# Fused attention and two MoE blocks: the x-combinations of the second block made one per product, a chunk ahead

## The chip, the cores and the metric

The kernel runs on one core of one Trainium2 chip. The metric is the device time of one execution in microseconds (us); the kernel before takes 1987.3 us, the median of three runs (1986.35 to 1988.73).

## The reference

```python
x = attention(q, k, v, p)              # 2304 tokens x 512, packed through 32 proxies
h = x @ w_in;  x = (h * cos(h)) @ w_out            # block 1, d_ff = 2048
P = sinkhorn(exp(x @ w_gate))                      # 2304 x 8, eight rounds
out = sum over e of P[:, e] * (relu(x @ w1[e]) @ w2[e])   # block 2: 8 experts, 1024 wide
```

All in float32. Each matrix is held as a rounded high part (`xh`, type fp32r) and a low part (`xl`, the difference), and every product is three matrix products (high*high, high*low, low*high).

## The kernel before, in words

Everything is transposed: features on the 128 partitions, tokens along the free dimension. After attention, block 1 runs as 64 steps `s` (four units of 16), written out in a fixed order: `in_front` and `in_back` issue for each step 12 matmuls of the first product (`in_g1`), the cosine on ScalarE (ACT) and VectorE (DVE) (`in_turns`, `in_rest`, `in_sin`, `in_square`, `in_g`), the split of h into high (`in_hi`, ACT) and low (`in_lo`, GpSimd, called POOL), the 24 matmuls of the second product for the step three before (`in_g2`), and its addition into the SBUF accumulator (`in_acc`, DVE, line 573). There are four pairs of PSUM banks, two for each product, so `in_g2(j)` waits for `in_acc(j-2)`.

Block 2 runs as 16 units (expert and half); u = 4 (`U1`) is the first. Tokens are cut into four chunks j of 512 columns (plus a rest, j = 4). In a chunk the first product uses a Strassen-Winograd scheme with seven products m in the order (0, 5, 1, 6, 4, 3, 2), each of 12 matmuls (`g1_mult`, line 723). They need seven combinations of blocks of x per chunk: m = 0, 1, 2 are plain blocks, m = 4, 5, 6, 3 are differences. `x_make(j, qs)` makes them: a subtraction on DVE (line 624), the high part on ACT (line 615), the low part on DVE or POOL (line 616), in staging slots (`slot_of`, 256-column pieces of `xh` and `xl` that block 1 no longer reads), and stores both parts to a DRAM tensor `xd` by two DMAs of the SP queue (line 618). `x_load` (line 656) loads the parts of a product from `xd` into a ring of four slots (0 to 3); it is called behind each product for the one four later, first four times ahead of the chunk loop. All 16 units read `xd`. The four blocks of w1 of a unit are combined and split in the same manner by `w1_make` on ACT and POOL (lines 678, 679, 682).

The generators are stepped by hand. In the kernel before, `x_make(0)` and `x_make(1)` are both stepped within steps 56 to 63 of block 1 and emptied behind them; `x_make(2)` and `x_make(3)` within chunk 0 and early chunk 1 of the first unit. Between the products of a chunk stand the second products: in chunk 0 of u = 4 the last three `in_g2` of block 1 (steps 61 to 63), then four `out_g2` per chunk (12 matmuls each, lines 827 to 829) of the chunk before. "Side" work, stepped by `step_side`, is the gate: `logits(c)` (matmuls line 863, copies 867 and 868, transposes 871, reduction 855, all in PSUM bank 7), and then `sinkhorn`. An engine's instructions run in the order in which they are written here.

Of the kernel before, what the change touches and what calls it, by code (L numbers as in the profile page):

```python
# [8 lines left out]
F32 = mybir.dt.float32  # L9
# [5 lines left out]
ALU = mybir.AluOpType  # L15
# [16 lines left out]
NJ = 4  # L32
# [71 lines left out]
def tile_kernel(ctx: ExitStack, tc: tile.TileContext, qT, kT, v, pT, w_in, w_out, w_gate, w1, w2, out):  # L104
# [496 lines left out]

    def x_make(j, qs):

        b11, b12 = x_block(0, 2 * j), x_block(0, 2 * j + 1)
        b21, b22 = x_block(1, 2 * j), x_block(1, 2 * j + 1)
        n = 0

        def tmp():
            return temp("tx").rearrange("p (a n) -> p a n", a=2)

        def put(m, src, eng):
            nonlocal n
            hi, lo = slot_of(qs[n % len(qs)])
            n += 1
            nc.scalar.copy(hi, src)  # L615
            eng.tensor_tensor(out=lo, in0=src, in1=hi.bitcast(F32), op=ALU.subtract)  # L616
            for i, part in enumerate((hi, lo)):
                nc.sync.dma_start(
                    out=xd[7 * j + m, :, i, :].rearrange("p (a n) -> p a n", a=2),
                    in_=part.bitcast(F32),  # L620
                )

        def sub(out, a, b):
            nc.vector.tensor_tensor(out=out, in0=a, in1=b, op=ALU.subtract)  # L624

        t1 = tmp()
        sub(t1, b12, b11)
        put(0, b11, nc.gpsimd)
        yield
        t2 = tmp()  # L630
        sub(t2, b22, t1)
        put(5, t2, nc.vector)
        yield
        put(1, b21, nc.gpsimd)
        put(4, t1, nc.vector)
        yield
        t3 = tmp()
        sub(t3, b22, b12)
        put(6, t3, nc.vector)
        yield  # L640
        t4 = tmp()
        sub(t4, b21, t2)
        put(3, t4, nc.vector)
        yield
        put(2, b22, nc.gpsimd)

    x_seq = [7 * j + m for j in range(NJ) for m in MULTS]
    counts = {"load": 0, "use": 0, "bank": 0, "slot": 0}

# [15 lines left out]
    def w1_make(u, early, late):  # L665
        def tile_():
            return wp.tile([P, 512], F32, tag="w1h", name="wraw")

        a11, a12, a21, a22 = (tile_() for _ in range(4))
        for i, t in enumerate((a11, a12, a21, a22)):  # L670
# [14 lines left out]
        put(0, a11, early[0])  # L685
        s1, s2 = tile_(), tile_()
        comb(s1, a21, a22, ALU.add)
# [242 lines left out]
    with tc.manual_schedule():  # L930
# [137 lines left out]

        def step_tail(n=1):
            for _ in range(n):  # L1070
                while tail:
                    try:
                        next(tail[0])
                        break
                    except StopIteration:
                        tail.pop(0)

        spare, late = [4, 5, 6, 7], [8, 9, 10, 11]
        preps = {U1: w1_make(U1, spare, late)}
        n0 = n1 - 16  # L1080
        for s in range(NPLAN, n1):
            in_front(s)
            in_back(s)
            if s == n0 + 4:
                w2_load(U1)
            if s == n0 + 7:
                next(preps[U1])
                w2_split(U1, 0)
            if s == n0 + 8:
                w2_split(U1, 1)  # L1090
                tail.append(x_make(0, range(4)))
            if s == n0 + 12:
                tail.append(x_make(1, range(4)))
            if n0 + 8 <= s < n0 + 15:
                step_tail(2)
            if n0 + 8 <= s < n0 + 13:
                next(preps[U1])
            if n0 + 13 <= s:
                next(preps[U1], None)
        step_tail(20)  # L1100
        next(preps[U1], None)
        for _ in range(4):
            x_load()
        tail.append(x_make(2, range(12, 16)))
        in_hi(n1 - 1)
# [9 lines left out]

        spare, late = [12, 13, 14, 15], [5, 7, 8, 10]
        prev = None
        for u in range(U1, NU):
            for j in range(NJ + 1):
                if prev is None:  # L1120
                    def last(i):
                        in_g2(i)
                        in_acc(i)
                        if i == n1 - 1:
                            tail.append(x_make(3, range(12, 16)))
                            side.extend(logits(c) for c in range(8))
                            side.extend([logits_rest(), sinkhorn()])
# [4 lines left out]
                steps = g1_steps(u, j) if j < NJ else g1_rest(u)  # L1132
                places = (1, 2, 3) if prev is None else (1, 3, 4, 5) if j < NJ else (0, 0, 1, 1)
                i = 0
                for n in range(7 if j < NJ else 2):
                    next(steps, None)
                    while i < len(g2) and places[i] == n:
                        g2[i]()
                        i += 1
                    step_tail(2 if prev is None and n < 4 else 1)  # L1140
                    if u > U1 or (j == 0 and n > 3) or (j > 0 and n in (1, 3, 4, 5)):
                        step_side()

                    if j == 0 and n in (3, 5):
                        w2_split(u, 2 + n // 5)
                    if u + 1 < NU:
                        if j == 1 and n == 0:
                            preps[u + 1] = w1_make(u + 1, spare, late)
                            next(preps[u + 1])
                        if j == 2 and n < 5:  # L1150
                            next(preps[u + 1])
# [56 lines left out]
```

## Time and profile before

| what | value |
|---|---|
| median of three runs | 1987.3 us |
| profiled execution | 1988.1 us, its span 1986.3 us |
| TensorE (PE) busy | 1936.6 us (97%), mean granted clock 0.991 |
| DVE, ACT, POOL busy | 961.3, 622.1, 530.1 us |
| DMA | 321.18 MB, mean 162 GB/s, 50.0% of 16 engines |

The span is the time from the first to the last instruction of the core; the execution's own time lies 1.8 us above it. PE busy 97% says that the matrix engine sets the end nearly everywhere, so time can only be won where it waits or where its clock is granted at half. The rows further below are from the 100 us in which block 1 ends and block 2 begins.

### The profile page before, as it was taken

The numbers are of one execution on the slowest core, as the hardware profiler recorded it, in microseconds if no ns is written. First come the engines' busy times: TensorE is split into PE (matmuls) and PEld (weight loads), VectorE is DVE, ScalarE is ACT, GpSimd is POOL, SyncE is SP. The second block draws the span as 40 slices with busy tenths as digits, with TensorE's granted clock in tenths as the row PEclk, the third lists the DMA queues.
The fourth block names the chain that finished last, engine by engine and source line by source line (L and its number), as shares of the span: only waits on it lengthen the run. The fifth ranks groups of instructions, "written<-read, shape, count | busy, mean of one in ns | idle before, by whom it ended". The sixth has DMA issues, their size and how long they took to land.

```text
span 1986.3 us, 32260 instructions
## 1 busy us (share of the span) xinstructions
PE 1936.6 (97%) x13241; PEld 1745.7 (88%) x13241; DVE 961.3 (48%) x1427; ACT 622.1 (31%) x1062; POOL 530.1 (27%) x426
## 2 busy tenths in 40 slices
PE   7999999869999999999999999999999999999998
PEld 4799999857889989998998989989989898989897
DVE  6867776653363554343444343434344444434343
ACT  5877776532321212121222121212111211212110
POOL 3445554642121212121212121213131222212100
PEclk9999999979999999999999999999999999999999
DMA  8411111385363737474646455555546463737373
GB/s 294 149 53 45 54 54 33 127 276 191 118 220 119 227 123 231 129 229 135 221 139 211 158 192 163 187 177 163 191 149 210 130 222 118 233 114 236 117 228 101
DMA packets 290067, 321.18 MB, mean 162 GB/s; under 512 B 18560, under 2 KB 267264, under 8 KB 289920
## 3 DMA queue, kind: packets, MB, share of 16 engines
q1 hardware_dynamic: 289920, 319.12, 50.0%
q8 instruction: 104, 1.70, 0.4%
q14 instruction: 43, 0.35, 0.1%
HBM read 299.65 MB, written 19.40 MB: 161 GB/s over the span
## 4 chain that ended last, share of the span: by engine, by line
PE 77%; DVE 1%; ACT 0%; issue 0%; DMA 0%; POOL 0%; SPq 0%; ACTq 0%
PE bank L723 32%; PE bank L827 13%; PE bank L828 13%; PE bank L829 13%; PE bank L792 5%; PE bank L863 0%; DMA xl<-xd 0%; DVE xl L616 0%; ACT xh L615 0%; DVE tx L624 0%; DVE c L747 0%; ACT hreg L731 0%; DVE lg L855 0%; POOL wlo L221 0%; DVE hreg L732 0%
## 5 line engine op out<-in xcount | busy, mean ns | idle before, releaser
L723 PE MATMUL bank<-xh 128*128 128x256 f32 x1792 | 509.5, 284 | 7.1 <-DMA xh<-xd 7.1
L723 PE MATMUL bank<-xl,xh 128*128 128x256 f32 x1792 | 507.6, 283 | 0.4 <-DMA xl<-xd 0.3
L723 PE MATMUL bank<-xh,xl 128*128 128x256 f32 x1792 | 507.6, 283 | 0.0
L839 DVE SCALAR_TENSOR_TENSOR acc<-bank,prob,acc 128x512 f32<-128x512 f32 (+1 forms) x253 | 189.5, 749 | 364.4 <-PE bank L829 364.1
L723 PEld LDWEIGHTS bank<-xh 128*128 128x128 f32 x1792 | 341.8, 191 | 22.0 <-issue 10.7
L723 PEld LDWEIGHTS bank<-xl,xh 128*128 128x128 f32 x1792 | 341.8, 191 | 10.3 <-DMA xl<-xd 0.9
L679 POOL TENSOR_TENSOR xl<-wraw,xh 128x512 fp32r<-128x512 f32 x128 | 165.1, 1305 | 684.6 <-ACT xh L678 471.4
L723 PEld LDWEIGHTS bank<-xh,xl 128*128 128x128 f32 x1792 | 342.3, 191 | 0.0
L827 PE MATMUL bank<-whi,hreg 128*128 128x512 f32 (+1 forms) x822 | 323.8, 394 | 0.0
L828 PE MATMUL bank<-wlo,hreg 128*128 128x512 f32 (+1 forms) x822 | 323.4, 393 | 0.0
L829 PE MATMUL bank<-whi,hreg 128*128 128x512 f32 (+1 forms) x822 | 322.8, 393 | 0.0
L731 ACT ACTIVATE hreg<-c 128x512 fp32r<-128x512 f32 x137 | 86.6, 632 | 459.7 <-DVE c L747 459.7
L221 POOL TENSOR_TENSOR wlo<-raw,whi 128x512 fp32r<-128x512 f32 x64 | 83.0, 1297 | 464.8 <-ACT whi L220 464.7
L562 PE MATMUL bank<-hreg,whi 128*128 128x288 f32 x1024 | 189.8, 297 | 7.5 <-DVE acc L573 7.0
L829 PEld LDWEIGHTS bank<-whi,hreg 128*128 128x128 f32 x822 | 154.6, 188 | 35.5
L827 PEld LDWEIGHTS bank<-whi,hreg 128*128 128x128 f32 x822 | 154.9, 188 | 28.0
L828 PEld LDWEIGHTS bank<-wlo,hreg 128*128 128x128 f32 x822 | 154.8, 188 | 27.2
L562 PEld LDWEIGHTS bank<-hreg,whi 128*128 128x128 f32 x1024 | 155.2, 191 | 10.2 <-ACT rbuf L524 4.2
L732 DVE SCALAR_TENSOR_TENSOR hreg<-c,hreg 128x512 fp32r<-128x512 f32 x137 | 97.6, 712 | 99.6 <-ACT hreg L731 99.6
L828 PE MATMUL bank<-wlo,slot 128*128 128x512 f32 (+1 forms) x334 | 131.0, 392 | 0.0
L827 PE MATMUL bank<-whi,slot 128*128 128x512 f32 (+1 forms) x334 | 131.0, 392 | 0.0
L829 PE MATMUL bank<-whi,slot 128*128 128x512 f32 (+1 forms) x334 | 130.4, 391 | 0.0
(152 smaller groups left out, 2828.1 us busy)
## 6 DMA issues: line engine op xcount, KB each, us to landing
xh<-xd SPq DMA_DIRECT2D x448, 256.0 KB, 3.4
xl<-xd SPq DMA_DIRECT2D x448, 256.0 KB, 3.8
raw<-w SPq DMA_DIRECT2D x32, 512.0 KB, 6.1
wraw<-w SPq DMA_DIRECT2D x64, 256.0 KB, 5.4
raw<-w_in SPq DMA_DIRECT2D x16, 512.0 KB, 3.8
raw<-w_out SPq DMA_DIRECT2D x16, 512.0 KB, 3.6
xd<-xh SPq DMA_DIRECT2D x28, 256.0 KB, 2.6
xd<-xl SPq DMA_DIRECT2D x28, 256.0 KB, 2.7
```

Source lines behind the costliest of these rows:

```text
L221: nc.gpsimd.tensor_tensor(out=lo, in0=raw, in1=hi.bitcast(F32), op=ALU.subtract)
L562: nc.tensor.matmul(ps[:, di, 0:HC], lhsT=lhsT, rhs=rhs, start=(n in (0, 6)), stop=(n in (17, 23)),)
L679: nc.gpsimd.tensor_tensor(out=lo, in0=src, in1=hi.bitcast(F32), op=ALU.subtract)
L723: nc.tensor.matmul(dst, lhsT=w, rhs=t[:, k, :], start=start and p + k == 0 and w is a and t is th, stop=p + k == 2 and w is bq, skip_group ...
L731: nc.scalar.activation(hi, src, AF.Relu)
L732: nc.vector.scalar_tensor_tensor(out=lo, in0=src, scalar=0.0, in1=hi.bitcast(F32), op0=ALU.max, op1=ALU.subtract)
L792: nc.tensor.matmul(dst, lhsT=w, rhs=t, start=q + k == 0 and w is a and t is th, stop=q == 1 and k == KD - 1 and w is bq, skip_group_check= ...
L827: nc.tensor.matmul(ps, lhsT=a, rhs=wh, start=(f == 0), stop=False)
L828: nc.tensor.matmul(ps, lhsT=a, rhs=wl, start=False, stop=False)
L829: nc.tensor.matmul(ps, lhsT=bq, rhs=wh, start=False, stop=(f == 3))
L839: nc.vector.scalar_tensor_tensor(out=dst, in0=ps, scalar=prob[:, t, e:e + 1], in1=dst, op0=ALU.mult, op1=ALU.add)
```

## The change

`x_make` keeps the same seven combinations, but each of its eight pieces finishes the low part of the product before and issues the next subtraction and high part; all low parts are now on DVE, none on POOL. `x_make(0)` is stepped once per step in steps 56 to 63, with its first four products written straight into ring slots 0 to 3 (they are still stored to `xd`), so that the load counter starts at 4 and the four loads ahead of the chunk loop are gone. `x_make(1)`, `(2)` and `(3)` are stepped one piece per product of chunks 0, 1 and 2 of the first unit, through slots 8 to 11, with their differences in buffers of the pool `wp`. The last four splits of the first `w1_make` move from the end of block 1 to products 0 to 3 of chunk 0, the next unit's `w1_make` from chunks 1 and 2 to chunks 2 and 3. The last three `in_g2` move from products 1, 2, 3 to 1, 3, 5, and in the first unit the side work is stepped at the last product of chunk 0 and then behind every product.

```diff
-    def x_make(j, qs):
+    def x_make(j, qs, tmp):
...
-        def put(m, src, eng):
-            nonlocal n
-            hi, lo = slot_of(qs[n % len(qs)])
-            n += 1
-            nc.scalar.copy(hi, src)
-            eng.tensor_tensor(out=lo, in0=src, in1=hi.bitcast(F32), op=ALU.subtract)
+        src = {0: b11, 1: b21, 2: b22}
+
+        def sub(m, a, b):
+            src[m] = tmp().rearrange("p (a n) -> p a n", a=2)
+            nc.vector.tensor_tensor(out=src[m], in0=a, in1=b, op=ALU.subtract)
+
+        def high(m):
+            nc.scalar.copy(slot_of(qs[m])[0], src[m])
+
+        def low(m):
+            hi, lo = slot_of(qs[m])
+            nc.vector.tensor_tensor(out=lo, in0=src[m], in1=hi.bitcast(F32), op=ALU.subtract)
             for i, part in enumerate((hi, lo)):
                 nc.sync.dma_start(
...
-        t1 = tmp()
-        sub(t1, b12, b11)
-        put(0, b11, nc.gpsimd)
-        yield
-        t2 = tmp()
-        sub(t2, b22, t1)
-        put(5, t2, nc.vector)
-        yield
-        put(1, b21, nc.gpsimd)
-        put(4, t1, nc.vector)
-        yield
...
+        sub(4, b12, b11)
+        high(0)
+        yield
+        low(0)
+        sub(5, b22, src[4])
+        high(4)
+        yield
+        low(4)
+        high(5)
+        yield
+        low(5)
+        sub(6, b22, b12)
+        high(1)
+        yield
+        low(1)
+        sub(3, b21, src[5])
+        high(6)
+        yield
+        low(6)
+        high(3)
+        yield
+        low(3)
+        high(2)
+        yield
+        low(2)
...
-    counts = {"load": 0, "use": 0, "bank": 0, "slot": 0}
+    counts = {"load": 4, "use": 0, "bank": 0, "slot": 0}
...
-        spare, late = [4, 5, 6, 7], [8, 9, 10, 11]
+        direct = {m: (0, 1, 2, 3, 8, 10, 9)[i] for i, m in enumerate(MULTS)}
+        through = {m: 8 + i % 4 for i, m in enumerate((0, 4, 5, 1, 6, 3, 2))}
+
+        def x_temp():
+            return wp.tile([P, 512], F32, tag="w1h", name="tx")
+
+        spare, late = [4, 5, 6, 7], [12, 13, 14, 15]
...
-                tail.append(x_make(0, range(4)))
-            if s == n0 + 12:
-                tail.append(x_make(1, range(4)))
-            if n0 + 8 <= s < n0 + 15:
-                step_tail(2)
+                tail.append(x_make(0, direct, lambda: temp("tx")))
+            if n0 + 8 <= s:
+                step_tail()
             if n0 + 8 <= s < n0 + 13:
                 next(preps[U1])
-            if n0 + 13 <= s:
-                next(preps[U1], None)
-        step_tail(20)
-        next(preps[U1], None)
-        for _ in range(4):
-            x_load()
-        tail.append(x_make(2, range(12, 16)))
...
+                first_unit = u == U1
+                if first_unit and 0 < j + 1 < NJ:
+                    tail.append(x_make(j + 1, through, x_temp))
...
-                            tail.append(x_make(3, range(12, 16)))
...
-                places = (1, 2, 3) if prev is None else (1, 3, 4, 5) if j < NJ else (0, 0, 1, 1)
+                places = (1, 3, 5) if prev is None else (1, 3, 4, 5) if j < NJ else (0, 0, 1, 1)
...
-                    step_tail(2 if prev is None and n < 4 else 1)
-                    if u > U1 or (j == 0 and n > 3) or (j > 0 and n in (1, 3, 4, 5)):
+                    if not first_unit or n == 6 or (j > 0 and n < 6):
                         step_side()
+                    if first_unit:
+                        if j == 0 and n < 4:
+                            next(preps[U1], None)
+                        step_tail()
...
-                        if j == 1 and n == 0:
+                        if (j, n) == ((2, 6) if first_unit else (1, 0)):
                             preps[u + 1] = w1_make(u + 1, spare, late)
                             next(preps[u + 1])
-                        if j == 2 and n < 5:
+                        if j == (3 if first_unit else 2) and first_unit <= n < 5 + first_unit:
                             next(preps[u + 1])
```

In `step_tail` every generator in the list now advances by one piece per call; before, only the first one did. In `w1_make` the six buffers are taken at once, in another order.

## Rows read from the trace of the kernel before

**Rows 1.** Waits, 350 to 450 us: who waited for whom, total us, times, longest.

```profile
PE bank L863 <- DVE lg L855: 7.4, 2, 3.9
PE bank L723 <- DMA xh<-xd: 7.1, 1, 7.1
PE bank L562 <- DVE acc L573: 7.0, 3, 3.2
PE bank L871 <- DVE l_rest L868: 4.6, 1, 4.6
```

**Rows 2.** Windows: length, busy per engine (x count), PEclk, DMA share, GB/s.

```profile
380.00:400.00 20.00, 12.93 (x81) 12.22 (x80) 14.06 (x17) 11.79 (x23) 11.11 (x12) 0.91 0.45 153
400.00:410.00 10.00, 5.57 (x24) 5.30 (x25) 5.15 (x6) 4.83 (x10) 8.70 (x8) 0.53 0.94 303
430.00:440.00 10.00, 5.13 (x24) 3.42 (x24) 4.96 (x11) 1.76 (x3) 1.53 (x2) 0.57 0.98 314
440.00:450.00 10.00, 6.18 (x35) 5.17 (x36) 3.14 (x8) 2.35 (x4) 0.85 (x1) 0.58 0.41 129
```

**Rows 3.** Timeline of PE: start us, us, line; first matmuls of steps 56 and 57.

```profile
347.64 0.29 PE L503 MATMUL bank<-xh 128*128 128x288 f32 x1
352.39 0.29 PE L503 MATMUL bank<-xh 128*128 128x288 f32 x1
```

**Rows 4.** Timeline of PE: chunk 0, its first two products, its third one.

```profile
404.34 0.55 PE L723 MATMUL bank<-xh 128*128 128x256 f32 x1 [7.13 <-DMA xh<-xd]
...
410.06 0.68 PE L562 MATMUL bank<-hreg,whi 128*128 128x288 f32 x2
...
413.61 0.28 PE L723 MATMUL bank<-xh 128*128 128x256 f32 x1
...
415.05 0.43 PE L562 MATMUL bank<-hreg,whi 128*128 128x288 f32 x2
```

**Rows 5.** Timeline of ACT: the copy behind the first product of chunks 1, 2, 3.

```profile
447.97 0.58 ACT L752 COPY ta<-bank 128x512 f32<-128x512 f32 x1 [5.06 <-PE bank L723]
...
475.07 0.59 ACT L752 COPY ta<-bank 128x512 f32<-128x512 f32 x1
...
498.52 0.59 ACT L752 COPY ta<-bank 128x512 f32<-128x512 f32 x1
```

**Rows 6.** Timeline of PE: an output, transposes, logits, next product.

```profile
456.50 0.40 PE L827 MATMUL bank<-whi,slot 128*128 128x512 f32 x1
...
459.27 0.38 PE L871 MATMUL bank<-ident,l_sb 128*128 128x128 f32 x2
459.96 0.69 PE L863 MATMUL bank<-acc,wgs 128*32 128x288 f32 x8 [0.32 <-DVE lg L855]
460.59 0.39 PE L723 MATMUL bank<-xh 128*128 128x256 f32 x1
```

**Rows 7.** Timeline of DVE: a logits copy, a low part behind ACT.

```profile
460.72 0.42 DVE L867 COPY l_sb<-bank 128x256 f32<-128x256 f32 x1 [0.81 <-PE bank L863]
...
463.70 0.69 DVE L732 SCALAR_TENSOR_TENSOR hreg<-c,hreg 128x512 fp32r<-128x512 f32 x1 [0.70 <-ACT hreg L731]
```

**Rows 8.** Lines 616 and 624: duration ns min/median/max, starts, forms.

```profile
L616 DVE TENSOR_TENSOR xl<-tx,xh x16: 691/693/1360, 357.2 to 442.9; 128x512 fp32r<-128x512 f32 x16
L616 POOL TENSOR_TENSOR xl<-acc,xh x12: 1262/1290/1747, 354.2 to 449.1; 128x512 fp32r<-128x512 f32 x12
...
L624 DVE TENSOR_TENSOR tx<-acc x8: 679/1029/1772, 353.1 to 433.1; 128x512 f32<-128x512 f32 x8
```

**Rows 9.** Three-microsecond window with a short wait, columns as in rows 2.

```profile
551.00:554.00 3.00, 1.54 (x13) 1.34 (x12) 2.57 (x8) 0.11 (x1) 0.00 (x0) 1.00 0.88 260
```

**Rows 10.** DMA issues, 410 to 440 us: count, KB each, median us to landing.

```profile
xd<-xl SPq DMA_DIRECT2D x12, 256.0 KB, 3.4
...
xl<-xd SPq DMA_DIRECT2D x6, 256.0 KB, 4.6
```

**Rows 11.** Tile xd, 395 to 470 us: issue to landing.

```profile
DMA to landing us min/median/max: 2.2/4.0/5.7
```

More of the change, by code (lines that the diff above doesn't have):

```diff
@@ L600, in x_block @@
         return cols.rearrange("p (a n) -> p a n", a=2)[:, :, 0:HT]
-    def x_make(j, qs):
+    def x_make(j, qs, tmp):
         b11, b12 = x_block(0, 2 * j), x_block(0, 2 * j + 1)
         b21, b22 = x_block(1, 2 * j), x_block(1, 2 * j + 1)
-        n = 0
-        def tmp():
-            return temp("tx").rearrange("p (a n) -> p a n", a=2)
-        def put(m, src, eng):
-            nonlocal n
-            hi, lo = slot_of(qs[n % len(qs)])
-            n += 1
-            nc.scalar.copy(hi, src)
-            eng.tensor_tensor(out=lo, in0=src, in1=hi.bitcast(F32), op=ALU.subtract)
+        src = {0: b11, 1: b21, 2: b22}
[7 more added lines that the diff above has]
+            nc.vector.tensor_tensor(out=lo, in0=src[m], in1=hi.bitcast(F32), op=ALU.subtract)
             for i, part in enumerate((hi, lo)):
@@ L621, in put @@
                 )
-        def sub(out, a, b):
-            nc.vector.tensor_tensor(out=out, in0=a, in1=b, op=ALU.subtract)
-        t1 = tmp()
-        sub(t1, b12, b11)
-        put(0, b11, nc.gpsimd)
+        sub(4, b12, b11)
+        high(0)
         yield
-        t2 = tmp()
-        sub(t2, b22, t1)
-        put(5, t2, nc.vector)
+        low(0)
+        sub(5, b22, src[4])
+        high(4)
         yield
-        put(1, b21, nc.gpsimd)
-        put(4, t1, nc.vector)
+        low(4)
+        high(5)
         yield
-        t3 = tmp()
-        sub(t3, b22, b12)
-        put(6, t3, nc.vector)
+        low(5)
+        sub(6, b22, b12)
+        high(1)
         yield
-        t4 = tmp()
-        sub(t4, b21, t2)
-        put(3, t4, nc.vector)
+        low(1)
+        sub(3, b21, src[5])
+        high(6)
         yield
-        put(2, b22, nc.gpsimd)
+        low(6)
[5 more added lines that the diff above has]
+        low(2)
     x_seq = [7 * j + m for j in range(NJ) for m in MULTS]
-    counts = {"load": 0, "use": 0, "bank": 0, "slot": 0}
+    counts = {"load": 4, "use": 0, "bank": 0, "slot": 0}
     def x_load():
@@ L667, in tile_ @@
             return wp.tile([P, 512], F32, tag="w1h", name="wraw")
-        a11, a12, a21, a22 = (tile_() for _ in range(4))
+        a11, s2, s1, a22, a12, a21 = (tile_() for _ in range(6))
         for i, t in enumerate((a11, a12, a21, a22)):
@@ L685, in w1_make @@
         put(0, a11, early[0])
-        s1, s2 = tile_(), tile_()
         comb(s1, a21, a22, ALU.add)
@@ L1067, in tile_kernel, with step_tail @@
         tail = []
[L1069 to L1076, printed above, removed]
-        spare, late = [4, 5, 6, 7], [8, 9, 10, 11]
+        def step_tail():
+            for make in list(tail):
+                if next(make, "end") == "end":
+                    tail.remove(make)
+        direct = {m: (0, 1, 2, 3, 8, 10, 9)[i] for i, m in enumerate(MULTS)}
[3 more added lines that the diff above has]
+        spare, late = [4, 5, 6, 7], [12, 13, 14, 15]
         preps = {U1: w1_make(U1, spare, late)}
@@ L1113, in tile_kernel @@
         l_rest = op.tile([P, 2 * P], F32, name="l_rest")
-        spare, late = [12, 13, 14, 15], [5, 7, 8, 10]
+        spare, late = [8, 9, 10, 11], [5, 7, 12, 14]
         prev = None
```

## The prediction

> **What bounds the kernel now.** I read the page first: PE is busy 97% of the span, and the row of granted clock over 40 slices is short of full only at the start and in slices 7 and 8, 347 to 447 us, where block 1 turns into block 2. So I asked only there, in this order: the waits of PE, the windows with the clock, then the timelines of PE, DVE and ACT side by side.
>
> The waits [rows 1] are four kinds, 26.1 us together: 7.0 on `in_acc` within block 1's last steps, 7.1 on the first load from `xd`, and 12.0 on the logits' reduction and copies on DVE. The reader is to see that DVE is not full there (14.06 of 20 us in the first of [rows 2]) and still late: `x_make` before issues a subtraction, a high part on ACT and a low part that needs it back to back, so DVE stands still within each piece, and two makes run at once. The windows [rows 2] show the second cost: behind waits of over 3 us the granted clock is 0.53, 0.57 and 0.58, near the lower of its levels (1.2 GHz), so PE needs about twice as long. The 24 matmuls behind the load take 5.72 us, later 12 take 1.44 [rows 4].
>
> After 500 us PE has hardly a gap and the change leaves the matmuls alone. All of the gain or loss lies between step 56 and the end of the first unit. I therefore place the new timeline against the old at four marks.
>
> **Mark 1, end of block 1.** A step is 4.75 us when nothing waits, and step 56 starts at 347.64 [rows 3]. Eight steps end at 347.6 + 8 x 4.75 = 385.6. Before, chunk 0 starts at 404.34 [rows 4], 18.7 us later. What is left in these steps: one make, four subtractions and seven low parts on DVE, 11 x 0.69 = 7.6 us [rows 8], 0.95 us per step, where there were two makes. Each low part needs a high part that ACT was given one piece earlier, so DVE doesn't stand still for it. The four loads are gone, and so is their 7.1 us: high and low of the first four products are in the ring already, the last of them (m = 6) from step 61. The 14 stores of the make still go to SP; nothing of chunk 0 waits for them but the loads of products 5 to 7, three to six products later. What hides the remaining work is each step's 4.75 us of PE; the gap next in line is `in_g2` of steps 62 and 63 on `in_acc`, which by the order on DVE comes out even with PE, to within half a microsecond. I allow 1.0 us.
>
> **Mark 2, chunk 0.** PE has seven products, 7 x 1.44 = 10.1 us [rows 4]; three `in_g2` of 24 of a step's 36 matmuls, 3 x 4.75 x 24/36 = 9.5 us [rows 3]; and logits(0), 0.69 [rows 6]: 20.3 us. DVE has five additions, four low parts of h, three `in_acc`, ten operations of `x_make(1)`, some 22 x 0.69 plus 0.6 for the copies [rows 7, 8] = 15.8 us, so PE stays the bound. In order, though, the last `in_acc` stands behind c21's addition, its high part on ACT and low part, and logits(0) needs its bank: it comes 1.3 us late by that order. So 21.6 us, and the copy that marks the first product of chunk 1 starts at 385.6 + 21.6 + 1.4 = 408.6. Before it starts at 447.97 [rows 5]: 39.4 us won so far.
>
> One cost isn't in that sum. The low parts move from POOL to DVE, and DVE's operations with both inputs in SBUF stretch when POOL works: the low part from 0.69 to 1.36 us, the subtraction from 0.68 to 1.77 [rows 8]. POOL still has seven operations of about 1.29 in chunk 0 (four w1 splits, two w2 splits, the last `in_lo`), 9 of 20 us. At best nothing meets. At worst all ten meet, 10 x 1.08 = 10.8 us, DVE 26.6 against PE's 20.3, 6.3 us over. At POOL's share it is 4.9 us, DVE 20.7: just even. I take 2.0 us. The Trainium skill (SBUF — State Buffer, Who interferes with whom) speaks harder against the move: a VectorE instruction with two SBUF inputs and a GpSimd one that reads SBUF exclude each other for the whole instruction. By that rule all ten would wait out a POOL operation, an estimate of 10 x 1.29 = 12.9 us, 2.1 more than by the rows, whose stretched operations of at most 1.77 bear a wait out but not always a whole one.
>
> **Mark 3, chunk 1.** Here the change costs. PE: 10.1 us of products, four outputs of 2.77 (456.50 to 459.27), and now seven side steps, not four, of 1.32 each (459.27 to 460.59, with a wait of 0.32) [rows 6]: 10.1 + 11.1 + 9.2 = 30.4 us. Behind products 2, 4, 5 and 6 of the scheme's order the output covers DVE; behind the first, third and last nothing does. There the reduction stands on DVE behind an addition (0.69), ACT's high part and a low part (0.70 and 0.69) [rows 7], and what `x_make` put ahead of it. Followed product by product, PE waits 1.5, 0.9 and 1.7 us more than the 0.32, with small change 4.5 us. At the least it is nothing (the 0.32 of the row), at the most three waits as long as the longest on the reduction before, 3 x 3.9 = 11.7 [rows 1]; I stay near the order's own sum because the make no longer has DVE wait inside a piece, which made the 3.9. So 34.9 us against 475.07 - 447.97 = 27.1 [rows 5]: 7.8 us lost.
>
> **Mark 4, chunk 2 and on.** Before, 498.52 - 475.07 = 23.45 [rows 5]. New: 10.1 + 11.1 + about 2 for the last logits and sinkhorn's first steps = 23.2, equal. The `sinkhorn` rounds, eight tiny matmuls and short DVE chains, come earlier by some products and end earlier; `w1_make` of the next unit runs two products behind its load and not seven, with ACT perhaps 1 us late, covered by the outputs. Both at nothing; if their cover fails, about 1 us each.
>
> DMA: stores and loads in chunks 0 to 2 are each 21 x 512 KB. In 410 to 440 us such a mix landed in 3.4 and 4.6 us [rows 10]. A store and the load behind it take 0.8 + 3.4 + 0.8 + 4.6 = 9.6 us with four issues of about 0.4; four products ahead is 4 x 1.44 and at least two outputs, 11.3 us. Hidden, with little to spare.
>
> **Sum.** 39.4 - 7.8 = 31.6 us, less 1.0 (steps), 2.0 (POOL) and 1.0 for a short fall of the clock: 27.6. The profiled execution took 1988.1 (span 1986.3 and 1.8 around it), so 1960.5; the median of the runs is 0.8 below that one: **1960**.
>
> **Rivals.**
> - *The clock falls in chunk 1.* Its waits come often, though none passes 2.0 us. For: waits of 3.2 to 7.1 [rows 1] were each followed by a low clock, and 430 to 450 stayed at 0.57 with 11.3 us of work in 20 [rows 2]. Against: in a window of 3 us with PE busy 1.54 the clock stayed 1.00 [rows 9]. Three falls as long as the 5.72 us of [rows 4] cost half of that each, 8.6: 1968. Through all of chunk 1 it is about 20: 1980.
> - *DVE becomes the bound*, in chunk 0 by the 6.3 us above and in the steps by some 4: 1960 - 3 + 10 = 1967. For: the 1.77 of [rows 8]. Against: POOL has nothing in chunk 1, and 9 of 20 us in chunk 0.
> - *The waits only move.* The stalls of chunk 0 on the logits (12.0 us, [rows 1]) and their clock (half of the 11.3 us in [rows 2]) come back in chunks 1 and 2, where the makes now run: 1960 + 17 = 1977. Against: DVE no longer waits inside a piece.
> - *Slower: stores and loads in a row on SP.* The load of products m = 5, 1, 6 stands on SP directly behind its store's issue, and must wait for it to land; the next store stands behind that wait. At the longest landing, 5.7 us [rows 11], a product takes 0.8 + 5.7 + 0.8 = 7.3 us of SP and PE gives it 4.2 (a product and an output). Three per chunk are then 3.1 each later, and the load's own landing adds: about 10 us per chunk, 30 over three: 1990. It decides when landings stay above some 4.5 us; the 3.4 of [rows 10], at a DMA share of over 0.9, speaks against. The Trainium skill (DMA: Bandwidth & Descriptors, Two DMAs through the same engine are not ordered) says that the issuing engine has to wait for the first DMA's semaphore; no row of before shows this wait by itself.
>
> **How the numbers follow.** Forecast, 1954 to 1966: 0.60. Better than 1954 (no contention, smaller waits): 0.05. Clock: 0.13. DVE: 0.11. Moved waits: 0.06. SP's row: 0.05. The range 1953 to 1976 leaves out the last two and the ends of the others. A measurement of this kernel tells about 0.2%, 4 us, from no change. Only SP's row, or the clock and DVE together, reach that band: faster 0.93, same 0.03, slower 0.04.
>
> **What would show it.** Right: the first product of chunk 0 near 386 us without a DMA wait, no wait of PE over 2.5 us after step 56, the copy of line 752 near 409, 444 and 467 us, granted clock 1.00 from 360 on. Low and subtraction durations in chunk 0 show the contention. Wrong: PE waiting on `xh<-xd` in chunks 1 to 3 (SP's row), a clock near 0.5 between 405 and 445, or chunk 1 longer than 40 us.

## The result, and the profile after

The changed kernel took 1966.68 us (median of four runs, 1966.26 to 1968.10) against 1986.93 before: a ratio of 0.990 (0.988 to 0.992), 20.3 us won of the 27 forecast. The profiled execution took 1966.81 against 1988.1, so 21.3 of a forecast 27.6. One execution of experiment 2 (2088.05 us) and one of experiment 9 (9058.42 us) were in a slower state, and no number below counts them. Line numbers behind 610 have changed: 723 is now 726, 752 is 755, 863 is 866, 855 is 858, 656 is 660; in `x_make`, 624 is 611 and 616 is 618.

The waits of PE, 340 to 480 us (total us, times, longest), answer to [rows 1]:

```profile
PE bank L866 <- DVE lg L858: 5.0, 7, 2.1
PE bank L866 <- DVE acc L573: 3.4, 1, 3.4
PE bank L726 <- DMA xl<-xd: 0.9, 1, 0.9
PE bank L562 <- DVE acc L573: 0.4, 1, 0.4
```

With two more of 0.3 and 0.2, the 26.1 us have become 10.2, over a longer stretch; one of 2.6 at 486 us comes below. The load's 7.1 is gone, and the 7.0 on `in_acc` inside block 1 is 0.4. What is new is 3.4 on `in_acc` in front of the logits. The windows, columns as in [rows 2], show the clock that went with it:

```profile
380.00:390.00 10.00, 10.00 (x80) 10.00 (x79) 7.01 (x11) 7.17 (x14) 3.56 (x5) 1.00 0.30 105
...
400.00:410.00 10.00, 6.64 (x54) 5.72 (x52) 6.49 (x10) 3.61 (x8) 3.25 (x3) 0.91 0.68 231
410.00:420.00 10.00, 9.37 (x53) 7.07 (x49) 5.41 (x12) 3.10 (x6) 1.29 (x1) 0.75 0.67 206
...
440.00:450.00 10.00, 7.28 (x50) 5.41 (x49) 4.20 (x11) 3.24 (x6) 0.00 (x0) 0.83 0.81 281
...
480.00:490.00 10.00, 7.14 (x34) 6.22 (x33) 4.96 (x11) 3.26 (x6) 5.30 (x5) 0.84 0.89 291
```

PE is full from 380 to 400 us (390 to 400 is 10.00 too), where it had been busy for 12.93 of 20 us, and no window is as low as the 0.53 to 0.58 of before. Four still lie well under 1.00. Their busy time times what the clock lacked (6.64 x 0.09 + 9.37 x 0.25 + 7.28 x 0.17 + 7.14 x 0.16) gives an estimate of 5.3 us for the lower clock.

ACT's copies behind the first product of chunks 0 to 3, and of the next unit, answer to [rows 5]:

```profile
390.57 0.58 ACT L755 COPY ta<-bank 128x512 f32<-128x512 f32 x1
413.16 0.58 ACT L755 COPY ta<-bank 128x512 f32<-128x512 f32 x1 [1.77 <-PE bank L726]
449.00 0.58 ACT L755 COPY ta<-bank 128x512 f32<-128x512 f32 x1 [4.09 <-PE bank L726]
472.21 0.57 ACT L755 COPY ta<-bank 128x512 f32<-128x512 f32 x1
517.07 0.59 ACT L755 COPY ta<-bank 128x512 f32<-128x512 f32 x1
```

From copy to copy, chunk by chunk:

| | chunk 0 | chunk 1 | chunk 2 | chunk 3 and rest |
|---|---|---|---|---|
| before | 40.2 | 27.1 | 23.45 | 38.6 |
| predicted | 21.6 | 34.9 | 23.2 | 38.6 |
| after | 22.6 | 35.8 | 23.2 | 44.9 |

Chunk 0 was also to begin earlier than it does by its copy: the first product starts at 386.01 (forecast 385.6), but its copy stands on ACT behind work of block 1's last step and comes at 390.57. So the forecast for chunk 0's end, 408.6, is the better test: 413.16. From its first product to that of chunk 1, chunk 0 takes 24.2 us where 21.6 was forecast.

**Where chunk 0 lost time.** The timelines of ACT, then DVE, then PE, each a fence (the bracket is the idle time before, and who ended it):

```profile
402.62 0.62 ACT L220 CAST whi<-raw 128x512 fp32r<-128x512 f32 x1 [2.24 <-PE bank L562]
403.14 0.63 ACT L734 ACTIVATE slot<-c 128x512 fp32r<-128x512 f32 x1
```
```profile
403.80 1.36 DVE L735 SCALAR_TENSOR_TENSOR slot<-c,slot 128x512 fp32r<-128x512 f32 x1 [2.82 <-ACT slot L734]
...
408.27 0.75 DVE L573 SCALAR_TENSOR_TENSOR acc<-bank,acc 128x576 f32<-128x576 f32 x1
```
```profile
386.01 0.28 PE L726 MATMUL bank<-xh 128*128 128x256 f32 x1
...
400.97 0.43 PE L562 MATMUL bank<-hreg,whi 128*128 128x288 f32 x2
...
409.07 1.19 PE L866 MATMUL bank<-acc,wgs 128*32 128x288 f32 x8 [3.36 <-DVE acc L573]
410.19 0.58 PE L726 MATMUL bank<-xh 128*128 128x256 f32 x1
```

Read it from the top, with the products of a chunk counted from one. The change moved the last `in_g2` from behind product 4 to behind product 6, where it starts at 400.97. Behind product 4 `w2_split(u, 2)` writes a buffer that this last `in_g2` has still to read, so ACT's rounding waits 2.24 us, into the middle of it. Behind the rounding on ACT stands the relu, DVE waits 2.82 us for that, `in_acc` is late, and PE waits 3.36 us. Then the logits take 1.19 us where they took 0.69, and the first matmul of chunk 1 takes 0.58 us where it took 0.39 [rows 6]: the lower of the two levels, 1.2 GHz.

**Where chunk 3 lost time.** ACT, PE and SP (durations on SP are those of issues):

```profile
483.04 0.62 ACT L682 CAST xh<-wraw 128x512 fp32r<-128x512 f32 x1 [6.46 <-DMA wraw<-w]
```
```profile
486.13 0.38 PE L726 MATMUL bank<-xh 128*128 128x256 f32 x1 [2.58 <-DMA xh<-xd]
```
```profile
465.05 0.36 SPq L660 DMA_DIRECT2D xh<-xd  x1
...
470.02 0.36 SPq L660 DMA_DIRECT2D xh<-xd  x1
...
474.89 0.36 SPq L660 DMA_DIRECT2D xh<-xd  x1
...
477.04 2.28 SPq L675 DMA_DIRECT2D wraw<-w  x4
479.41 0.38 SPq L660 DMA_DIRECT2D xh<-xd  x1
```

SP's loads of x follow each other at 4.9 us, where PE takes 4.2 us for a product and an output. SP's waits, 460 to 480 us, say why: three loads wait, some 3 us each, for a store to land, each for that of its own product, issued right ahead.

```profile
SPq L660 <- DMA xd<-xh: 9.1, 3, 3.5
```

The DMA share over 455 to 480 us, in 40 slices, has holes in step with these waits, so the DMA engines are not full; it is the row of SP that is serial:

```profile
DMA  9989999998779961019589940189998102879999
```

On top come the next unit's four w1 loads, 2.28 us of issue in front of the load at 479.41. ACT, meanwhile, waits 6.46 us for those w1 tiles with a relu behind it, and PE waits 2.58 for x.

### The profile page after: what moved, and what is told of

It is laid out like the page before. It is cut to its first block, busy times and chain, and to the rows that moved or that the text cites. A ratio compares the mean times of both kernels' runs of the same rounds, so it can differ in the third digit from the quotient of the medians.

```text
span 1965.0 us, 32232 instructions
## 1 busy us (share of the span) xinstructions
PE 1929.4 (98%) x13241; PEld 1739.3 (89%) x13241; DVE 964.8 (49%) x1439; ACT 621.7 (32%) x1062; POOL 516.4 (26%) x414
## 4 chain that ended last, share of the span: by engine, by line
PE 93%; DVE 2%; ACT 2%; DMA 1%; issue 1%; POOL 1%; SPq 0%; ACTq 0%; DVEq 0%; POOLq 0%
PE bank L726 32%; PE bank L830 13%; PE bank L831 13%; PE bank L832 13%; PE bank L562 9%; PE bank L795 5%; PE bank L503 1%; PE bank L505 1%; PE bank L504 1%; PE bank L440 1%; DMA xl<-xd 1%; DMA k<-kT 1%; PE bank L866 0%; DVE xl L618 0%; DMA xd<-xl 0%
## 5 line engine op out<-in xcount | busy, mean ns | idle before, releaser
L831 PEld LDWEIGHTS bank<-wlo,hreg 128*128 128x128 f32 x822 | 155.0, 189 | 27.1
```

The lines of the kernel that those rows point to most:

```text
L831: nc.tensor.matmul(ps, lhsT=a, rhs=wl, start=False, stop=False)
```

## The experiments

All edits are to the changed kernel. Runs of one kernel lie up to 6 us apart (8.5 in the last), so the stages, copy to copy as above, tell more than the medians; each stage is of one profile. Step 56 begins at 346.8 to 349.6 us in these profiles, before any edit acts, so clock times of two versions can differ by that much for no reason of the edit.

**1. The second half of w2 two products later.**

```diff
-                    if j == 0 and n in (3, 5):
-                        w2_split(u, 2 + n // 5)
+                    if j == 0 and n in ((5, 6) if first_unit else (3, 5)):
+                        w2_split(u, (n - 3 if first_unit else 2 + n // 5))
```

> Of the changed kernel alone: the splits of the first unit's third and fourth w2 block move from products 4 and 6 of chunk 0 to products 6 and 7, behind the last in_g2. Theory A (chunk 0 is 4.6 us longer than forecast because ACT stands 2.2 us on the copy of line 220, whose buffer the last in_g2 still reads, and everything behind it in ACT and DVE order comes late, up to the logits' wait of 3.4 us and the half clock behind it): the wait on acc before the logits falls to at most 1.5 us, the copy of line 755 in chunk 1 comes 4 to 5 us earlier, 1962 us. Rival B (POOL stretches DVE in chunk 0, or DVE has too much there): the two splits run on POOL a little later, DVE is as late as before, 1966 to 1967 us.

1966.10 us (1963.57 to 1966.53), ratio 0.989 (0.988 to 0.991). Stages 18.5, 37.1, 23.0, 46.3. PE's timeline has the logits behind a wait of 0.58, not 3.36:

```profile
406.54 0.69 PE L866 MATMUL bank<-acc,wgs 128*32 128x288 f32 x8 [0.58 <-DVE acc L573]
```

So the split of w2 is the cause in chunk 0, worth 4.1 us there. Chunks 1 and 3 gave 2.7 of it back, and the time doesn't tell the two kernels apart: theory A had the wait, but not its 1962.

**2. The next unit's w1 loads earlier** (in chunk 1, as before the change; the makes' temporaries get tiles of their own for it).

```diff
-            return wp.tile([P, 512], F32, tag="w1h", name="tx")
+            return op.tile([P, 512], F32, tag="tx", name="tx", bufs=3)
...
-                        if (j, n) == ((2, 6) if first_unit else (1, 0)):
+                        if (j, n) == (1, 0):
```

> Of the changed kernel alone: the next unit's four w1 loads are issued at the first product of chunk 1 (as in the kernel before), not at the last product of chunk 2; so that they can be, the differences of x_make(1) to (3) lie in three buffers of their own. The splits stay in chunk 3. Theory A (chunk 3 is 6.3 us longer than before because 1 MB of w1 lands among the stores and loads of x, so that ACT stands 6.5 us on its first split and PE 3.8 us on loads of x): both waits go, chunk 3 and the rest take 38.5 to 39.5 us instead of 44.9, 1961 us. Rival (the loads of x are late by their own stores, on SP, whatever w1 does): ACT's wait goes, PE's 3.8 us stay, 1965 us.

1961.56 us (median of three, 1961.52 to 1964.22), 0.987 (0.985 to 0.989). Stages 22.6, 36.0, 23.0, 40.4: chunk 3 alone changed, by 4.5 us. PE's waits on x, 385 to 520 us:

```profile
PE bank L726 <- DMA xh<-xd: 0.8, 1, 0.8
PE bank L726 <- DMA xl<-xd: 0.7, 1, 0.7
```

So 4.5 of the 6.3 us that the prediction had "at nothing" go with the place of these four loads; the edit also gives the temporaries other buffers, and no run tells the two apart.

**3. The gate's steps at four places of a chunk, not six or seven.**

```diff
-                    if not first_unit or n == 6 or (j > 0 and n < 6):
+                    if not first_unit or (j == 0 and n == 6) or (j > 0 and n in (1, 3, 4, 5)):
```

> Of the changed kernel alone: from chunk 1 on the first unit's side work is stepped only behind the four products with an output, as before, and not behind all seven. Theory A (behind products without an output PE waits for the logits' reduction, 1.3 and 2.1 us in chunk 1, and the clock falls behind the last): chunk 1 shrinks from 35.8 to 26.5 to 28 us, chunk 2 grows from 23.2 to 27, the clock stays at 1.00 there, 1962 us. Rival (the stores and loads of x set the pace of chunk 1, PE only waits elsewhere): waits on loads of x take the place, chunk 1 stays over 32 us, 1967 us or more.

1968.34 us (1964.20 to 1970.00), 0.990. Stages 20.9, 28.1, 32.7, 44.5. Chunk 1 gets back 7.7 us, where the prediction had 7.8 for its extra steps and their waits. Chunk 2 loses 9.5. PE's and ACT's waits, 385 to 520 us:

```profile
PE bank L726 <- DMA xh<-xd: 4.2, 2, 2.1
...
PE bank L726 <- DMA xl<-xd: 2.4, 5, 0.8
```
```profile
ACT xh L614 <- DMA xd<-xh: 21.4, 6, 6.2
```

With chunk 1 shorter, the staging slots are still being stored when ACT wants them, and x comes late. The wait moved; it did not go: chunk 1 came out nearly as theory A had it, the time as the rival had it.

**4. The first four products of chunk 0 loaded from DRAM again** (`counts["load"]` 0, and four `x_load()` behind block 1).

```diff
-    counts = {"load": 4, "use": 0, "bank": 0, "slot": 0}
+    counts = {"load": 0, "use": 0, "bank": 0, "slot": 0}
...
+        for _ in range(4):
+            x_load()
```

> Of the changed kernel alone: the first four products are loaded from xd as in the kernel before, by four loads issued behind the last store of x_make(0); the parts that lie in the ring already are loaded over by the same values. Theory (what the in-place part is worth is the wait for that load and the half clock behind it): chunk 0 starts 8 to 10 us later with a DMA wait of that length, then some 2.5 us of half clock, less what DVE and ACT catch up meanwhile: 1974 to 1978 us. Rival (the gain is from the make being one and not two, and the in-place part only hides a load that is early anyway): the loads land within 4 us, 1968 us.

1976.39 us (1972.45 to 1977.71), 0.994 (0.993 to 0.996). PE waits again in front of chunk 0:

```profile
396.64 0.55 PE L726 MATMUL bank<-xh 128*128 128x256 f32 x1 [9.13 <-DMA xh<-xd]
```

The first product starts 9.3 us later than after, counted from step 56, and the time is 9.7 longer: making four in place is worth that much. It is about half of what the change wins.

**5. As 3, with the stores of makes 1 to 3 in GpSimd's queue.**

```diff
-                nc.sync.dma_start(
+                (nc.gpsimd if j else nc.sync).dma_start(
```

> The kernel with four side steps per chunk, and the stores of x_make(1) to (3) issued from POOL's queue and not from SP's. In the four-step run what chunk 1 won came back in chunk 2 as waits on loads of x (6.6 us), ACT's waits on staging slots whose store had not landed (3.3, 3.7, 6.2 us) and half clock. Theory C (on SP a load stands behind its store and the next store behind that load, so stores are issued late): stores go out when their low part is done, the waits of ACT on xd<-xh and of PE on loads of x fall to under half, 1961 to 1963 us. Rival D (the 16 DMA engines are full in chunks 1 and 2, whoever issues): the waits stay, 1967 to 1969 us.

1965.88 us (1961.30 to 1967.50), 0.989. Stages 23.1, 27.5, 30.8, 42.8. Waits on x fall from 6.6 to 4.9 us, ACT's on the slots from 21.4 in six to 7.3 in four. SP's row is a part of the wait, not all of it: chunks 2 and 3 became shorter by about 2 us each, chunk 0 longer by 2.2, and the runs of the two, with medians 2.5 us apart, overlap.

**6. Makes 1 to 3 four products earlier** (make 1 from step 60).

```diff
+            if s == n0 + 12:
+                tail.append(x_make(1, {0: 11, ...}, lambda: temp("tx")))
...
-                if first_unit and 0 < j + 1 < NJ:
-                    tail.append(x_make(j + 1, through, x_temp))
...
+                        if j < 2 and n == 3:
+                            tail.append(x_make(j + 2, through, x_temp))
```

> Of the changed kernel alone: x_make(1), (2) and (3) start four products earlier (x_make(1) at step 60 of block 1, the others at product 4 of chunks 0 and 1), so that each store has four products more to land. Theory (chunks 1 to 3 wait because product, store and load follow each other too closely, while DMA is idle before): the waits on loads of x and on the w1 loads in chunk 3 go, chunk 3 takes 39 to 41 us and not 44.9, block 1's last steps stretch by at most 2 us, 1960 to 1962 us. Rival (DVE and ACT have no room in block 1's last steps with two makes): waits on acc there of 3 us or more, 1967 us or more.

1965.82 us (1963.95 to 1966.13), 0.989. No wait on x is left, and chunk 3 takes 38.8 us, the 38.6 of before. But two makes now run at once in block 1's last steps, and ACT's timeline shows the price:

```profile
395.57 0.24 ACT L580 CAST xh<-acc 128x64 fp32r<-128x64 f32 x1 [3.05 <-DVE acc L573]
395.72 0.58 ACT L755 COPY ta<-bank 128x512 f32<-128x512 f32 x1
```

The copy comes 5.2 us later than after, and PE waits 2.6 for it. Chunk 3 wins 6.0 us, but chunk 2 begins 4.3 later, so most of that is given away before, and the time lies between the two forecasts.

**7. Edits 1 and 2 together.** No other line is changed.

> The edits of the first two runs together (w2 splits behind the last in_g2, w1 loads in chunk 1). Theory F (the two delays lie in different chunks and don't share a resource): 3.9 us in chunk 0 and 4.4 us in chunk 3, 1958 to 1960 us. Rival G (chunks 1 to 3 follow the stores and loads of x, so what chunk 0 wins is given back there, as the first run gave back 2.7 of 3.9 us): 1961 to 1963 us, with more waits of ACT on staging slots or of PE on loads of x than in the second run.

1964.77 us (1962.61 to 1967.56), 0.989. Stages 18.5, 37.2, 23.0, 45.3. Chunk 0 is as in 1, but chunk 3 is not as in 2. ACT's waits, 400 to 520 us:

```profile
ACT xh L614 <- DMA xd<-xh: 11.5, 5, 5.4
```

The two gains don't add, and the time is above both forecasts: the wait for the stores has grown (2.6 after) in the place of the one for w1. That a shorter chunk 0 brings it, as a shorter chunk 1 does in 3, is argued, not shown.

**8. The pieces of a make back to back again** (subtraction, high and low part of one product in one piece).

```diff
-        sub(4, b12, b11)
-        high(0)
-        yield
-        low(0)
-        sub(5, b22, src[4])
-        high(4)
-        yield
-        low(4)
-        high(5)
-        yield
...
+        sub(4, b12, b11)
+        put(0)
+        yield
+        put(4)
+        yield
+        sub(5, b22, src[4])
+        put(5)
+        yield
...
```

> Of the changed kernel alone: each piece of x_make holds the subtraction, the high part on ACT and the low part of one product back to back, as the kernel before had it, all else (one make at a time, a piece per product, all low parts on DVE, in place) as changed. The forecast said that the waits before came from DVE standing still inside a piece. Theory: each piece has DVE wait 0.7 to 1.4 us for ACT, in chunk 1 the logits' reduction comes later behind each product without an output; the waits on line 858 grow from 5.0 to 8 to 12 us, the clock falls oftener, 1972 to 1978 us. Rival (the pace of one piece per product is what helped): 1966 to 1968 us.

1970.87 us (1967.65 to 1971.62), 0.992 (0.990 to 0.993), 4.2 above after, with stages 24.2, 38.2, 24.7, 42.5. PE's wait on the logits' reduction, 345 to 520 us (lines from 650 on are three lower here), then DVE's for the high parts, 350 to 450 us, here and before the change:

```profile
PE bank L863 <- DVE lg L855: 5.8, 7, 2.9
```
```profile
DVE xl L618 <- ACT xh L614: 10.3, 12, 1.4
```
```profile
DVE xl L616 <- ACT xh L615: 13.7, 16, 3.3
```

After the change DVE has no such wait, so the prediction was right that it stood still inside a piece. But the split into pieces is worth only some 4 us, less than the theory had (its wait on the logits, 5.8 and not 8 to 12) and more than the rival: chunks 0 to 2 lose 5.5, and chunk 3, with each store a piece earlier, wins 2.4.

**9. The low parts of m = 0, 1, 2 on POOL again.**

```diff
-            nc.vector.tensor_tensor(out=lo, ...)
+            (nc.gpsimd if m < 3 else nc.vector).tensor_tensor(out=lo, ...)
```

> Of the changed kernel alone: the low parts of the plain blocks (m = 0, 1, 2) on POOL, as before; the others stay on DVE. The forecast took 2.0 us for POOL stretching the low parts that moved to DVE. Theory E (DVE's load and its stretching by POOL cost PE those 2 us): 1964 to 1965 us. Rival (DVE has room, and a low part on POOL takes 1.3 us and not 0.7, and stretches DVE's other operations): 1966 to 1968 us.

1967.70 us (median of three, 1962.97 to 1968.31), 0.990 (0.988 to 0.991): no gain that shows, as the rival had it. No trace of these executions is kept, so only the time speaks.

**10. Edits 1, 2 and 6 together.** No other line is changed.

> The two edits, and x_make(1) to (3) four products earlier. Rival G expects the earlier stores to pay now that chunk 0 is shorter: no wait on loads of x, 1 to 3 us under the kernel with two edits. Theory F expects the 2.6 us wait and the later start of chunk 0 that the lead alone showed, and no wait left for it to remove: 1 to 4 us over it.

1963.29 us (1961.52 to 1966.48), 0.989. Stages 19.2, 39.1, 22.7, 38.9 and, as in 6, a copy at 395.87. Chunk 3 is short, and no wait on x is left; chunk 1 is 3.2 us longer than after. The median is 1.5 below 7, as rival G had it, but the runs overlap.

**11. As 7, with the gate's steps at five places.**

```diff
-                    if not first_unit or n == 6 or (j > 0 and n < 6):
+                    if not first_unit or (j == 0 and n == 6) or (j > 0 and 0 < n < 6):
```

> The same two edits, and in chunks 1 to 3 of the first unit no side step behind the first and the last product. Theory F: chunk 1 has two side steps (2.6 us) and the longest wait (2.1 us) and half clock behind it less, two steps come back in chunk 2: 2 to 3 us under the kernel with two edits. Rival G: a shorter chunk 1 gives the stores less time, waits on loads of x come in chunks 1 and 2, no gain or a loss of 1 to 2 us, as with four side steps.

1968.18 us (1965.67 to 1969.80), 0.991. Stages 18.5, 34.9, 27.1, 42.2. PE's waits, 400 to 520 us:

```profile
PE bank L866 <- DVE lg L858: 9.5, 7, 5.4
```

Chunk 2 takes over more than chunk 1 gave up. The time is 3.4 above 7, but by waits on the logits and not, as rival G had it, on x (1.7 us, 4.2 in 7).

**12. As 1, with each make in the order of use** (pieces 0, 5, 1, 6, 4, 3, 2), so that no load stands right behind its own store.

```diff
-        high(4)
-        yield
-        low(4)
         high(5)
         yield
         low(5)
-        sub(6, b22, b12)
         high(1)
...
-        through = {m: 8 + i % 4 for i, m in enumerate((0, 4, 5, 1, 6, 3, 2))}
+        through = {m: 8 + i % 4 for i, m in enumerate((0, 5, 1, 6, 4, 3, 2))}
```

> The second half of w2 later (as in e1), and in every chunk's making the pieces in the order of use (0, 5, 1, 6, 4, 3, 2, not 0, 4, 5, 1, 6, 3, 2), so that products 5, 1 and 6 of chunks 1 to 3 are stored one product earlier and no load stands on SP right behind its own store. Theory H (SP's chain store, landing, load sets the pace of chunk 3: 4.9 us per product in the changed kernel and in e7, against 4.2 of TensorE work): SP's loads follow each other at no more than 4.3 us in chunk 2's second half, the x wait in chunk 3 goes, chunk 0 is 18 to 19 us as in e1, chunk 3 at most 41 from copy to copy where e1 has 46.3, and the time is 1958 to 1962. Rival D (the 16 DMA engines or the wait for the w1 tiles set it, the order of SP's work does not): chunk 3 stays at 44 to 47, and the time is 1965 to 1967. Slower than 1968 would say that DVE's later low parts hold up chunk 0.

1962.81 us (1961.12 to 1969.57), 0.989 (0.987 to 0.990). Stages 18.4, 38.9, 23.0, 40.7. PE's largest wait on x, 400 to 520 us, and SP's own waits, 458 to 475 us:

```profile
PE bank L726 <- DMA xh<-xd: 1.5, 1, 1.5
```
```profile
SPq L620 <- DVE xl L618: 5.7, 2, 3.5
SPq L660 <- DMA xd<-xh: 1.9, 2, 1.4
```

Chunk 3 falls by 5.6 against 1, as theory H has it, and is under its 41. SP's wait for its own stores is 1.9 us and not 9.1; it now waits for DVE, which makes what is stored. In the second half of chunk 2 the loads follow each other at 2.8 and 4.7 us, where H said at most 4.3; the next, behind a store that waits for DVE and the w1 loads, comes 7.4 later. The median lies between the two forecasts. The w1 loads are where they were, so SP's order by itself takes back most of what chunk 3 had lost; so does moving the w1 loads in 2. Both ease the same row of SP.

From step 56 to the fourth copy of the next unit, one profile each (us):

| before | after | 1 | 2 | 3 | 4 | 5 | 6 | 7 | 8 | 10 | 11 | 12 |
|---|---|---|---|---|---|---|---|---|---|---|---|---|
| 251.5 | 230.1 | 228.6 | 225.7 | 230.7 | 237.9 | 229.8 | 227.6 | 227.6 | 234.2 | 228.3 | 231.7 | 225.5 |

Edits 2, 10 and 12 have the lowest medians, 5.1, 3.4 and 3.9 us below after. All three runs of 2 lie under the four of after, and in this stretch 2 and 12 are some 4.5 us shorter. But the intervals of their ratios overlap with that of after, so no version here is shown to be faster than the changed kernel. Edit 12 with 2 wasn't tried.

## Why the prediction was right, and where its sizes were off

**The mechanism held.** The gain lies where it was put, between step 56 and the end of the first unit, and the marks account for it. Against the forecast of 27.6 for the profiled execution: chunk 0's end 4.6 us late, against 4.0 taken off for steps, contention and clock (-0.6); chunk 1 0.9 longer; chunk 2 equal; chunk 3 and rest 6.3 longer; the next unit up to its fourth copy 1.7 shorter (60.3 against 62.0, nowhere in the sum). That makes 21.5, and 21.3 was measured. Taken out one at a time, making four in place is worth 9.7 us (experiment 4) and the split into pieces 4.2 (8). One make instead of two beside block 1, the places of `in_g2` and those of the w1 splits have no run of their own; 6, with two makes again from step 60, shows only that the second one costs there.

**Where the number was lucky.** The 4.0 us taken off for steps, contention and clock nearly meet the 4.6 by which chunk 0 ends late, but most of the 4.6 is the wait on the last `in_acc`, whose cause the prediction did not have, and the lower clock behind it. The next unit then gave 1.7 us that were not forecast. The time itself, 1966.7, lies just outside the forecast's own 1954 to 1966, beside the rivals of DVE (1967) and of the clock (1968); the stages tell them apart, not the time. Of the signs of being right, the first product at 386 came; three did not, with waits of 3.4 and 2.6 us, a clock under 1.00 and the copies 4 to 5 us late. One sign of being wrong came, PE waiting for `xh<-xd` in front of a product of chunk 3. (The page's clock row is short in its ninth slice alone, not in the places that the prediction read; nothing rests on it.)

**Mark 1, right.** 386.01 against 385.6, without a DMA wait, PE busy 10.00 of 10; the eight steps took 38.7 us against 38.0. Experiment 4 gives the loads their price, 9.7 where [rows 1] had 7.1.

**Mark 2, the wait on the last `in_acc`: 1.3 predicted, 3.4 measured.** The order on DVE had been followed, the buffers that ACT writes had not: `w2_split` was not in the list of what stands by the `in_g2` that moved. 20.3 of PE work, 3.4 of wait and 0.5 for logits at half clock are the 24.2 us from the first product of chunk 0 to that of chunk 1. Experiment 1 shows the cause.

**POOL's contention: 2.0 taken, 1.2 measured on the ten operations counted, some 0.7 on the path.** DVE's subtractions and low parts between 352 and 410 us, grouped (busy, mean ns):

```profile
L618 DVE TENSOR_TENSOR xl<-tx,xh 128x512 fp32r<-128x512 f32 x7 | 5.3, 758 | 0.0
L611 DVE TENSOR_TENSOR tx<-acc 128x512 f32<-128x512 f32 x4 | 4.8, 1204 | 0.0
L618 DVE TENSOR_TENSOR xl<-acc,xh 128x512 fp32r<-128x512 f32 x5 | 4.2, 849 | 0.0
L611 DVE TENSOR_TENSOR tx<-acc,tx 128x512 f32<-128x512 f32 x4 | 4.2, 1054 | 0.0
```

Twenty operations took 18.5 us; at 0.69 they are 13.8. DVE lost 4.7 us, most of it in block 1's steps, where PE waited 0.4 us for it; the ten of `x_make(1)` in chunk 0 lost 1.2. What the count left out are the low parts of h, which have both inputs in SBUF too: the one at 403.80, on the way to the late `in_acc`, takes 1.36 us and not 0.69, beside this operation of POOL:

```profile
403.31 1.29 POOL L221 TENSOR_TENSOR wlo<-raw,whi 128x512 fp32r<-128x512 f32 x1 [1.78 <-ACT whi L220]
```

The Trainium skill (SBUF — State Buffer, Who interferes with whom) says that a DVE operation with two SBUF inputs and a POOL operation that reads SBUF shut each other out for a whole instruction. The trace agrees: POOL's ends at 404.60, DVE's 0.56 us later, at 405.16; the stretched subtraction at 390.30 ends 0.55 us behind POOL's of 389.90. So DVE loses what is left of an operation that POOL had begun; the prediction's estimate of 12.9 us took ten meetings with a whole one; five of the ten were stretched, and only one by more than 0.2 us. Experiment 9 took low parts off DVE and won nothing that shows.

**The clock: 1.0 taken, about 5 lost.** "None passes 2.0 us" was said of chunk 1, where 2.1 came; 3.4 in front of it and 2.6 in chunk 3 came as well, and each of the three was followed by matmuls at the lower level. The rival of three falls was right in kind, at an estimated 5 us and not 8.6; the first begins in front of chunk 1, and the last is in chunk 3.

**Mark 3, right, with one part for another.** 35.8 against 34.9, and experiment 3 gives back 7.7 against 7.8. Behind the third and the last product PE waits 1.0 and 1.8 us more than 0.32, as forecast (0.9 and 1.7); behind the first it waits no more than 0.32, where 1.5 was forecast, and an estimated 2 us of lower clock stand there instead (its first product takes 2.73 us where 1.44 is the full clock's). That nothing else could be won there was not in the prediction: a shorter chunk 1 takes away the time in which stores and loads go by.

**Mark 4, chunk 2 right, "both at nothing" wrong by 6.3.** The w1 loads, two products ahead of their use, hold SP for 2.28 us in front of a load that is already late, and ACT for 6.46; the cover that the prediction named, the outputs, was too short. The stores and loads that it called "hidden, with little to spare" were compared by their latency; the row of SP sets a pace as well. With the loads moved, chunk 3 is 40.4; with the makes early (6, 10), 38.8 and 38.9, as before. The rival of SP's row had the mechanism, and its price of 30 us was too high: the wait for a store was some 3 us, not the 5.7 of [rows 11], so a product took 4.9 us of SP and not 7.3. Its threshold does not follow from its own sum: with 4.2 us per product and two pairs of issues of 0.8, SP falls behind when the wait passes 2.6 us, not 4.5.

**The next unit, 1.7 us, not foreseen.** The last of `sinkhorn`'s small matmuls (line 914) stands at 533.4 us; before (line 911) it stood at 577.6, inside the second chunk of that unit, which takes 19.9 us where it took 22.2. In 11, where it stands at 556.8, inside that chunk again, the chunk takes 22.7.

**Why a shorter chunk 0 gave some back.** In 1, 7, 10 and 12 a chunk 0 of 18.4 to 19.2 us was followed by a chunk 1 of 37.1 to 39.1, where 35.8 stands after. In each, POOL's low parts of the moved w2 splits now lie beside DVE operations in front of the logits' copies and reduction. Experiment 1, POOL, DVE, then PE:

```profile
407.88 1.29 POOL L221 TENSOR_TENSOR wlo<-raw,whi 128x512 fp32r<-128x512 f32 x1 [0.62 <-ACT whi L220]
```
```profile
408.38 1.34 DVE L735 SCALAR_TENSOR_TENSOR hreg<-c,hreg 128x512 fp32r<-128x512 f32 x1 [0.70 <-ACT hreg L734]
```
```profile
410.20 0.44 PE L874 MATMUL bank<-ident,l_sb 128*128 128x128 f32 x2 [1.37 <-DVE l_rest L871]
411.58 1.19 PE L866 MATMUL bank<-acc,wgs 128*32 128x288 f32 x8 [0.94 <-DVE lg L858]
```

The second low part meets DVE's next one in the same way (1.32 us). The order in time is plain: two stretched operations of DVE, two waits of PE, and only then matmuls at the lower level (1.19 us for the logits, 0.83 granted between 410 and 420). What stays open is what a place for these splits clear of both would win; no run has one.

## What to carry to other kernels

When a step moves, list what writes each buffer that it reads as well as who computes what it needs: here the next weights' rounding, not the arithmetic of the moved step, set the end of chunk 0. A store that is read back through the same sequencer has a pace of its own (issue, landing, issue); compare it with the pace of the consumer before shortening what lies beside it, and keep other loads out of that row. And place the new timeline at marks: here they showed that two removals of waits, each real in its stage, bought less together (2.5 us of the stretch above) than one of them alone (4.5).

## What the runs showed that was not expected

A wait of about 2 us can be followed by the lower clock or not. The changed kernel, and then experiment 1, PE's timeline with the window around it:

```profile
445.31 0.79 PE L866 MATMUL bank<-acc,wgs 128*32 128x288 f32 x8 [2.09 <-DVE lg L858]
```
```profile
444.06 0.69 PE L866 MATMUL bank<-acc,wgs 128*32 128x288 f32 x8 [2.09 <-DVE lg L858]
```
```profile
440.00:450.00 10.00, 7.59 (x60) 6.35 (x57) 6.52 (x16) 2.28 (x5) 0.00 (x0) 1.00 0.84 273
```

The wait is the same and the PE busy time nearly (7.28 and 7.59 of 10); the granted clock is 0.83 in the one and 1.00 in the other. The same wait is followed by 0.84 in 2 and by 1.00 in 7. So a clock term for waits of this length can be bounded by rows, and not forecast from their length alone.
